# A linear-attention and two-mixer kernel: clamps on GpSimd, an earlier third tile, low parts by TensorE and ScalarE

## The chip, the cores and the metric

One core of a Trainium2 chip runs the whole program. The metric is the device time of one execution in microseconds, as the median of several runs. The five engines are TensorE (PE; its weight loads are listed as PEld), VectorE (DVE), ScalarE (ACT), GpSimd (POOL) and SyncE (SP), which issues the DMAs.

## The reference

The program has three parts. The first is a linear attention with decay: 4 batches, 8 heads, 768 steps, head size 48. The second is a mixer with a convolution over three steps and a gate. The third is a normalised residual mixer. All of it is in 32-bit floats.

```python
for t in range(S):
    cur = np.einsum('bhd,bhe->bhde', u[None] * kt, vt)
    y[:, :, t] = np.einsum('bhd,bhde->bhe', rt, state + cur)
    state = w[None, :, :, None] * state + np.einsum('bhd,bhe->bhde', kt, vt)
# then, on x of 4 x 768 x 384
h = np.maximum(x @ w_in, 0.0)                      # 384 -> 1024
conv_out[s] = sum over k of conv_w[k] * h[s + k - 1]
x = h * sigmoid(conv_out) @ w_out                  # 1024 -> 384
xn = (x - mean) / sqrt(var + 1e-6) * g_ln
out = x + np.maximum(xn @ w_ch1, 0.0) @ w_ch2      # 384 -> 1536 -> 384
```

## The kernel before

**Tiles.** The attention runs over 24 tiles of 128 steps, six for each batch. Inside a tile it is turned into matrix products: `dps` are the dot products of keys and queries, `aT` is their masked copy, `pst` is the tile's part of the state, `sbds` is the state laid out for TensorE, and `yps` is the tile's result, transposed, in one PSUM bank. The first mixer takes eight blocks of three tiles (`mixer1`), the second six blocks of four (`mixer2`).

**Three products for one.** TensorE multiplies in a shorter float format (fp32r). So each operand is split into a high part and a low part, and each product is made of three matmuls: high by high, high by low, low by high. For a tile's result, ScalarE copies `yps` to `xh` (the rounding makes the high part), and then the low part `xl` is `yps - xh`. Tiles 4 and 5 already make `xl` in another way: TensorE adds `-1 * xh` to the same bank (the matrix `minus`), and ScalarE copies the rest out.

**Weights.** The weights are split in the same way, but a program makes their rounding by hand, since they come in a packed form of two words: `magnitude` (line 122) has ScalarE take the absolute value and another engine clamp it; `decode` (line 129) has VectorE shift and merge bits in three steps; then ScalarE writes the high part and VectorE the low part. These steps are the generator `steps` of a weight job; `wdo(count)` advances the current job by so many steps (line 211), and a step that ends decoding calls the next job's `ahead`, so that the next magnitude is made early. Jobs 0 to 2 and 4 to 6 are parts of `w_in` (512 columns each), jobs 3, 7, 8 and 9 parts of `w_out` (768), and later jobs belong to the second mixer. Line 155 decides which engine clamps: VectorE for jobs 0 to 9, GpSimd from job 10 on.

**What sets the order.** A planner orders the instructions of each engine by its own costs, except those that are issued through `pe`, `vo`, `ao`, `go` and `so`: these keep the program's order on their engine. All matmuls, all of decoding with its ScalarE steps, and all of the first four tiles (`EARLY`) are of this kind; their line in the profile is the helper's, 77. In later tiles, ScalarE's and VectorE's steps are mostly left to the planner. An engine works its list strictly one after the other.

**The start.** `startup` (line 435) is written out by hand: `on(n)` runs the next part of tile n, `state_sum`, `state_update` and `decayed` do the state and the decayed keys, and `wdo` decodes weights between them. A light tile (n < 6) has four parts: the products `rk` and `z` on VectorE; dot products, mask and copies; `yps` and the `xh` copy; the low part and the halos. The others have three: `rk`, sums and `aT`; dot products and the masked copy; `yps`, `xh`, `xl` and the loads. After the start, `attention` (line 464) is a generator whose `go_on(n)` runs the next part of tile n; the first mixer advances it between its blocks of matmuls.

**PSUM.** The tag `pa` has three banks. `dps` (two), `yps` and `pst` of tiles from 4 on take turns in them.

Of the kernel before, what the change touches and what calls it, by code (L numbers as in the profile page):

```python
# [8 lines left out]
F32 = mybir.dt.float32  # L9
F32R = mybir.dt.float32r  # L10
I32 = mybir.dt.int32
AF = mybir.ActivationFunctionType
ALU = mybir.AluOpType
# [23 lines left out]
EARLY = 4  # L37
HAND = 9
LIGHT = 6
STEPS = (2, 4, 6, 8, 10, 12, 15), (1, 3, 4, 6, 7, 9, 10, 12, 14, 16)  # L40
GC = 16
GE = 4
# [8 lines left out]
def body(ctx, tc, r, k, v, w, u, w_in, conv_w, w_out, g_ln, w_ch1, w_ch2, rkT, krv, small, out):  # L51
# [13 lines left out]
    v_ = nc.vector  # L65
    a_ = nc.scalar
# [55 lines left out]
    def magnitude(st, n, engine=go):  # L122

        t = ap.tile([128, WN], F32, tag="wd", name="wdec", bufs=2)[:, 0:n]
        ao.activation(out=t, in_=words(st, n)[1].bitcast(F32), func=AF.Abs)
        engine.tensor_scalar(out=t, in0=t, scalar1=W_MIN, scalar2=W_MAX, op0=ALU.max, op1=ALU.min)
        return t
# [14 lines left out]
    def wjob(src, n, hi, lo, scale=None):  # L142

        st, mag = [], []

        def load():
            st.append(io.tile([128, 2 * WN], I32, tag="st" if me >= 4 else "first", name="st", bufs=3 if me >= 4 else 4))
            dst = st[0][:, 0:2 * n]
            if len(src.shape) == 3:
                dst = dst.rearrange("p (a n) -> p a n", a=src.shape[1])  # L150
            so.dma_start(out=dst, in_=src.bitcast(I32))

        def ahead():
            if not mag:
                mag.append(magnitude(st[0], n, vo if me < 10 else go))

        def steps():
            ahead()
            t = mag[0]
            yield from decode(st[0], n, t)  # L160
            if me + 1 < min(len(wjobs), w_loaded[0]):
                wjobs[me + 1][2]()
            if len(src.shape) == 3:
                t = t.rearrange("p (a n) -> p a n", a=src.shape[1])
            kw = {} if scale is None else {"scale": gl[:, scale:scale + 1]}
            ao.activation(out=hi, in_=t, func=AF.Copy, **kw)
            yield
            if scale is None:
                vo.tensor_tensor(out=lo, in0=t, in1=hi.bitcast(F32), op=ALU.subtract)
            else:  # L170
                vo.scalar_tensor_tensor(out=lo, in0=t, scalar=kw["scale"], in1=hi.bitcast(F32),
                                        op0=ALU.mult, op1=ALU.subtract)
        me = len(wjobs)
        wjobs.append((load, steps(), ahead))
        return len(wjobs) - 1

# [76 lines left out]
    def decayed_k(n):  # L253

        if n < LIGHT:
            vo.tensor_tensor(out=kks[:, n % 2, 0, :, 0:D], in0=loaded[n][1], in1=tku[:, 0], op=ALU.mult)
            return
        inputs(n).tensor_tensor(out=kks[:, n % 2, :, :, 0:D], in0=loaded[n][1].unsqueeze(1).to_broadcast([128, 2, H, D]), in1=tku,
                         op=ALU.mult)
# [29 lines left out]
    def halos(n, xh, xl):  # L289
        i, j = n % TPB, n // TT  # L290
        g_ = vo if n < EARLY else nc.gpsimd
        for t, e in ((xh, 0), (xl, 1)):
            if i == 0:
                g_.memset(t[:, :, 0:1].bitcast(F32), 0.0)
            if i == TPB - 1:
                g_.memset(t[:, :, T + 1:T + 2].bitcast(F32), 0.0)
            if n % TT == 0 and i > 0:
                g_.tensor_copy(out=xT[j - 1][e][:, :, T + 1:T + 2], in_=t[:, :, 1:2].bitcast(F32))
                g_.tensor_copy(out=t[:, :, 0:1], in_=xT[j - 1][e][:, :, T:T + 1].bitcast(F32))
# [68 lines left out]
    def attn_tile(n):  # L368
        b, i = divmod(n, TPB)
        rk, _, rt, vt, _ = loaded[n]  # L370
        py, py_tag = (ps_c, "acc") if n < EARLY else (ps_a, "pa")

        rT, kT = rk[:, 0], rk[:, 1]
        vo.tensor_tensor(out=rk, in0=rk, in1=trk, op=ALU.mult)
        if n < LIGHT:
            yield from light_tile(n, rk, vt, py, py_tag)
            return
        av = ap.tile([128, H, D], F32, tag="av", name="av", bufs=2)
        v_.tensor_tensor(out=av, in0=kks[:, n % 2, 1, :, 0:D], in1=rt, op=ALU.mult)
        a8 = sp.tile([128, H, 1], F32, tag="a8", name="a8", bufs=2)  # L380
        v_.tensor_reduce(out=a8.rearrange("x (q p) o -> x q (p o)", q=2), in_=av.rearrange("x (p q) d -> x q p d", q=2),
                         axis=AX.X, op=ALU.add)
        aT = ap.tile([128, 2, NP, C], F32, tag="aT", name="aT", bufs=2)
        for h in range(H):
            a_.activation(out=aT[:, h // NP, h % NP, :], in_=ident, func=AF.Copy, scale=a8[:, h, :])
        yield

        dps = dot_products(rT, kT)
        for q in range(2):
            v_.copy_predicated(out=aT[:, q], mask=later.bitcast(I32).unsqueeze(1).to_broadcast([128, NP, C]), data=dps[q])  # L390
        yield

        yps = py.tile([128, KT, C], F32, tag=py_tag, name="yps")
        products(n, yps, rT, vt, aT)
        j = n // TT
        xh, xl = xT[j] if j in xT else new_xT(j)
        sl = slice(1 + (n % TT) * C, 1 + (n % TT) * C + C)
        a_.activation(out=xh[:, :, sl], in_=yps, func=AF.Copy)
        v_.tensor_tensor(out=xl[:, :, sl], in0=yps, in1=xh[:, :, sl].bitcast(F32), op=ALU.subtract)
        load_tile(n + 3)  # L400
        if n + 2 < NT:
            decayed_k(n + 2)
        halos(n, xh, xl)
        finished[0] = n
        yield
# [3 lines left out]
    def state_sum(n):  # L409
        vt = loaded[n][3]  # L410
        if n % TPB != TPB - 1:
            pst = sums[n] = ps_a.tile([128, NP, D], F32, tag="pa", name="pst")
            for h in range(H):
                q0 = 64 * (h % 2)
                pe.matmul(pst[q0:q0 + 64, h // 2, :], lhsT=kks[:, n % 2, 0, h, :], rhs=vt[:, h, 0:D], start=True,
                          stop=True)

    def state_update(n):
        first, last = n % TPB == 0, n % TPB == TPB - 1
        v_, a_, g_ = ordered(n)  # L420
        if not last:
            pst = sums.pop(n)
            sn = ap.tile([PR, NP, D], F32, tag="sn", name="sn")
            if first:
                a_.activation(out=sn, in_=pst[0:PR], func=AF.Copy)
            else:
                v_.tensor_tensor(out=sn, in0=pst[0:PR], in1=state[0], op=ALU.add)
            if n % TPB < TPB - 2:
                state[0] = ap.tile([PR, NP, D], F32, tag="sw", name="sw")
                v_.tensor_tensor(out=state[0], in0=sn, in1=w128.to_broadcast([PR, NP, D]), op=ALU.mult)  # L430
            sb = sbd[(n + 1) % 2]
            a_.activation(out=sb[0:D, :, 0:D], in_=sn[0:D], func=AF.Copy)
            a_.activation(out=sb[64:PR, :, D:2 * D], in_=sn[64:PR], func=AF.Copy)

    def startup():

        tiles = {n: attn_tile(n) for n in range(EARLY + 1)}

        def on(n):
            next(tiles[n], None)  # L440

        decayed = decayed_k
        on(0), decayed(0), on(0)
        on(1), state_sum(0), state_update(0), decayed(1), on(1), state_sum(1)
        wdo(1)
        on(0), on(2), state_update(1), decayed(2)
        wdo(2)
        on(2), state_sum(2), on(0)
        wdo(1)
        on(1), on(3), state_update(2), decayed(3)  # L450
        wdo(2)
        on(3), state_sum(3), on(1)
        wdo(2)
        on(2), state_update(3)
        wdo(3)
        on(2), on(3)
        wdo(1)
        on(3)
        wdo(1)
        on(4), decayed(4)  # L460
        wdo(3)
        return tiles

    def attention(tiles):

        def go_on(n):
            if 0 <= n < NT:
                next(tiles.setdefault(n, attn_tile(n)), None)

        n = EARLY  # L470
        load_tile(n + 2)
        decayed_k(n + 1)
        go_on(n)
        yield
        for n in range(EARLY, NT):
            state_sum(n)
            state_update(n)
            go_on(n - 1)
            if n != LIGHT - 1:
                go_on(n + 1)  # L480
            yield
            go_on(n)
            if n == LIGHT - 1:
                yield
                go_on(n)
                go_on(n + 1)
                yield
            go_on(n + 1)
            yield

    def split_T(x, n, hi, lo, c0):
# [456 lines left out]
```

## Time and profile before

| | |
|---|---|
| median of 3 runs | 653.33 us |
| lowest and highest | 652.41 and 654.55 us |
| the profiled execution's own time | 653.91 us |
| its span, first to last instruction | 652.2 us |
| TensorE busy | 627.9 us, 96% of the span |
| VectorE busy | 421.7 us, 65% |
| ScalarE busy | 300.8 us, 46% |
| GpSimd busy | 81.2 us, 12% |
| the chain that ended last | TensorE 84%, VectorE 10%, ScalarE 2% |

The shares are means over very different stages. In the first hundred microseconds the attention's small steps, the weights' decoding and the first mixer run together; later there is little else than matmuls. So the profile is read by stages: busy times of each engine in windows, then the chain of waits, and then single instructions in order of time. A matmul's end is modelled; the spacing of starts tells more than its duration. PEclk is the share of TensorE's clock that was granted, 1.00 for 2.4 GHz and 0.5 for 1.2 GHz.

### The profile page before, as it was taken

The page shows a single profiled execution, that of the slowest core. Times are in us where ns is not written, and L with a number is a line of the kernel's source. Part 1 is how long each engine was busy: PE and PEld are TensorE (multiplying, and loading weights), DVE is VectorE, ACT ScalarE, POOL GpSimd, SP SyncE. Part 2 cuts the span into 40 slices and gives each one's busy share as a digit, 9 for nine tenths or more (in the row PEclk, how much of TensorE's full clock was granted, in tenths as well). Part 3 has the DMA queues.
Part 4 walks back from the last instruction along what each step waited for, and adds up shares of the span by engine and source line. Part 5 has one row for each costly group of instructions (what it writes and reads, how often), then busy time and mean ns, then how long its engine had stood idle before and what let it go on. Part 6 is the DMA issues. An engine that isn't in the chain of part 4 may idle for free.

```text
span 652.2 us, 11821 instructions
## 1 busy us (share of the span) xinstructions
PE 627.9 (96%) x4803; PEld 572.3 (88%) x4803; DVE 421.7 (65%) x793; ACT 300.8 (46%) x658; POOL 81.2 (12%) x108
## 2 busy tenths in 40 slices
PE   8969879999999999999999999999999999999996
PEld 5768868889999999999999999999999999999995
DVE  6989999999989999968978834314213422422111
ACT  3447677687687877766755511211211211211110
POOL 6312010110020001002115501001000100100000
PEclk8867989999999999999999999999999999999999
DMA  8934644444253524012125103002002001100001
GB/s 231 309 107 156 211 146 125 125 133 159 71 174 118 162 83 137 18 47 88 52 82 171 60 0 98 1 0 98 1 0 83 16 0 50 50 0 19 31 0 54
DMA packets 25296, 56.52 MB, mean 87 GB/s; under 512 B 2961, under 2 KB 15378, under 8 KB 25234
## 3 DMA queue, kind: packets, MB, share of 16 engines
q1 hardware_dynamic: 25234, 55.68, 27.1%
q8 instruction: 40, 0.66, 0.4%
q14 instruction: 22, 0.18, 0.1%
HBM read 46.24 MB, written 9.44 MB: 85 GB/s over the span
## 4 chain that ended last, share of the span: by engine, by line
PE 84%; DVE 10%; ACT 2%; issue 1%; DMA 1%; POOL 1%; SPq 0%; DVEq 0%; ACTq 0%; POOLq 0%
PE acc L77 36%; PE psm L77 36%; PE yps L77 5%; PE dps L77 4%; DVE wdec L77 3%; DVE c L541 2%; PE pst L77 2%; PE pxt L77 1%; DVE rk L77 1%; DMA x1b<-x_dram 1%; DVE c L522 1%; PE pa L77 1%; DVE gl L528 1%; DVE kks L77 0%; POOL tables L762 0%
## 5 line engine op out<-in xcount | busy, mean ns | idle before, releaser
L555 DVE SCALAR_TENSOR_TENSOR rl<-psm,rh 128x512 fp32r<-128x512 f32 x72 | 49.6, 689 | 136.0 <-ACT rh L554 132.5
L554 ACT ACTIVATE rh<-psm 128x512 fp32r<-128x512 f32 x72 | 43.1, 599 | 199.6 <-PE psm L77 199.5
L77 PE MATMUL acc<-c2h,rh 128*128 128x384 f32 x288 | 97.0, 337 | 0.0
L77 PE MATMUL acc<-c2l,rh 128*128 128x384 f32 x288 | 97.0, 337 | 0.0
L77 PE MATMUL acc<-c2h,rl 128*128 128x384 f32 x288 | 96.9, 336 | 0.0
L77 PE MATMUL psm<-xnh,c1h 128*128 128x512 f32 x216 | 86.6, 401 | 0.0
L77 PE MATMUL psm<-xnh,c1l 128*128 128x512 f32 x216 | 84.9, 393 | 0.0
L77 PE MATMUL psm<-xnl,c1h 128*128 128x512 f32 x216 | 84.7, 392 | 0.0
L541 DVE SCALAR_TENSOR_TENSOR c<-h,tables,c 128x384 f32<-128x384 f32 x128 | 78.5, 617 | 8.0 <-ACT c L539 7.5
L77 PE MATMUL psm<-xh,wih 128*128 128x386 f32 x192 | 69.8, 364 | 4.4 <-DVE xl L77 4.4
L77 PE MATMUL acc<-woh,gl 128*128 128x384 f32 x192 | 65.3, 340 | 4.4 <-DVE gl L528 4.4
L77 PE MATMUL acc<-woh,gh 128*128 128x384 f32 x192 | 67.4, 351 | 0.4 <-ACT gh L527 0.4
L77 PE MATMUL psm<-xl,wih 128*128 128x386 f32 x192 | 67.1, 350 | 0.0
L77 PE MATMUL psm<-xh,wil 128*128 128x386 f32 x192 | 66.9, 348 | 0.0
L77 PE MATMUL acc<-wol,gh 128*128 128x384 f32 x192 | 65.3, 340 | 0.0
L77 PEld LDWEIGHTS acc<-c2l,rh 128*128 128x128 f32 x288 | 54.0, 188 | 3.0
L77 PEld LDWEIGHTS acc<-c2h,rh 128*128 128x128 f32 x288 | 54.1, 188 | 2.8
L77 PEld LDWEIGHTS acc<-c2h,rl 128*128 128x128 f32 x288 | 54.0, 188 | 0.0
L77 PEld LDWEIGHTS psm<-xnh,c1l 128*128 128x128 f32 x216 | 40.6, 188 | 9.3
L77 POOL TENSOR_SCALAR wdec<-wdec 128x768 f32<-128x768 f32 (+1 forms) x13 | 35.7, 2749 | 103.4 <-ACT wdec L77 76.3
L77 PEld LDWEIGHTS psm<-xnl,c1h 128*128 128x128 f32 x216 | 40.6, 188 | 6.1
L77 PEld LDWEIGHTS psm<-xnh,c1h 128*128 128x128 f32 x216 | 40.6, 188 | 6.1
(132 smaller groups left out, 1107.9 us busy)
## 6 DMA issues: line engine op xcount, KB each, us to landing
rk<-in_rkT_dram SPq DMA_DIRECT2D x24, 448.0 KB, 4.5
st<-in_moe_w_ch_dram SPq DMA_DIRECT2D x12, 768.0 KB, 4.6
rv<-in_krv_dram SPq DMA_DIRECT2D x18, 448.0 KB, 4.7
kt<-in_krv_dram SPq DMA_DIRECT2D x24, 192.0 KB, 4.5
x_dram<-x SPq DMA_DIRECT2D x24, 192.0 KB, 1.9
x1b<-x_dram SPq DMA_DIRECT2D x24, 192.0 KB, 3.3
out_dram<-x1b SPq DMA_DIRECT2D x24, 192.0 KB, 2.0
st<-in_moe_w_in_dram SPq DMA_DIRECT2D x6, 512.0 KB, 9.4
```

What stands on the lines that cost most here:

```text
L77: return lambda *args, **kw: tc.keep_in_program_order(op(*args, **kw))
L522: v_.tensor_tensor(out=st["c"], in0=st["h"][:, 1:T + 1], in1=st["c"], op=ALU.mult)
L528: v_.tensor_tensor(out=st["gl"], in0=st["c"], in1=st["gh"].bitcast(F32), op=ALU.subtract)
L541: v_.scalar_tensor_tensor(out=c, in0=h[:, o:o + T], scalar=cw[:, tap, f:f + 1], in1=c, op0=ALU.mult, op1=ALU.add)
L554: a_.activation(out=gh[:, 0:cols], in_=ps[:, 0:cols], func=AF.Relu)
L555: v_.scalar_tensor_tensor(out=gl_[:, 0:cols], in0=ps[:, 0:cols], scalar=0.0, in1=gh[:, 0:cols].bitcast(F32), op0=ALU.max, op1=ALU.subtract)
```

## The change

There are three edits. The clamps of weight jobs 6 to 9 go from VectorE to GpSimd. In `startup`, the third part of tile 0 (`yps`, `xh`) and the first part of tile 2 (`rk`, `z`) are put ahead of the first step of the first weight job. Tiles 6 to 9 make their low part as tiles 4 and 5 do, by the matrix `minus` and a ScalarE copy; this is a fourth part of the tile, which `attention` runs right behind the second part of the next tile.

```diff
+MID = 10
@@ wjob, ahead
-                mag.append(magnitude(st[0], n, vo if me < 10 else go))
+                mag.append(magnitude(st[0], n, vo if me < 6 else go))
@@ attn_tile
         a_.activation(out=xh[:, :, sl], in_=yps, func=AF.Copy)
-        v_.tensor_tensor(out=xl[:, :, sl], in0=yps, in1=xh[:, :, sl].bitcast(F32), op=ALU.subtract)
         load_tile(n + 3)
         if n + 2 < NT:
             decayed_k(n + 2)
+        if n < MID:
+            yield
+            pe.matmul(yps, lhsT=minus, rhs=xh[:, :, sl], start=False, stop=True, skip_group_check=True)
+            a_.activation(out=xl[:, :, sl], in_=yps, func=AF.Copy)
+        else:
+            v_.tensor_tensor(out=xl[:, :, sl], in0=yps, in1=xh[:, :, sl].bitcast(F32), op=ALU.subtract)
         halos(n, xh, xl)
@@ startup
         on(1), state_sum(0), state_update(0), decayed(1), on(1), state_sum(1)
+        on(0), on(2)
         wdo(1)
-        on(0), on(2), state_update(1), decayed(2)
+        state_update(1), decayed(2)
         wdo(2)
@@ attention
             go_on(n + 1)
+            if LIGHT <= n < MID:
+                go_on(n)
             yield
```

## Rows read from the trace of the kernel before

**Rows 1.** Windows: length, busy us of PE, PEld, DVE, ACT, POOL; PEclk, DMA, GB/s.
```profile
20.00:40.00 20.00, 15.19 (x267) 12.52 (x263) 18.42 (x35) 11.12 (x25) 6.19 (x8) 0.89 0.78 234
60.00:80.00 20.00, 18.21 (x144) 17.43 (x143) 20.00 (x32) 13.96 (x26) 2.53 (x3) 0.93 0.56 181
80.00:100.00 20.00, 16.13 (x148) 14.40 (x149) 19.30 (x34) 13.24 (x34) 2.85 (x3) 0.91 0.47 146
200.00:220.00 20.00, 20.00 (x226) 18.87 (x225) 18.87 (x34) 14.43 (x38) 0.21 (x2) 1.00 0.48 152
```

**Rows 2.** Chain of waits, 13 to 45 us: start, us, engine and tile.
```profile
19.65 0.49 ACT xh L77
...
21.51 0.43 DVE wdec L77
...
40.11 3.25 PE psm L77 x9
```

**Rows 3.** Timeline of TensorE: start, us, engine, line, instruction [idle before <-releaser].
```profile
80.14 1.16 PE L77 MATMUL dps<-rk 48*128 48x128 f32 x16 [1.93 <-ACT c L539]
...
89.70 0.45 PE L77 MATMUL acc<-woh,gl 128*128 128x384 f32 x1 [3.30 <-DVE gl L528]
```

**Rows 4.** Timeline of ScalarE and VectorE, 15 to 20 us.
```profile
15.38 0.68 ACT L77 ACTIVATE wdec<-st 128x512 f32<-128x512 f32 x1
...
16.09 0.99 DVE L77 TENSOR_SCALAR wdec<-wdec 128x512 f32<-128x512 f32 x2 [2.89 <-ACT wdec L77]
...
17.00 1.22 DVE L77 TENSOR_TENSOR rk<-rk,tables 112x1024 f32<-112x1024 f32 x1
...
18.93 0.35 DVE L77 TENSOR_TENSOR sn<-pst,sw 112x192 f32<-112x192 f32 x1
...
19.65 0.49 ACT L77 ACTIVATE xh<-yps 128x384 fp32r<-128x384 f32 x1 [3.60 <-PE yps L77]
...
20.06 1.41 DVE L77 SCALAR_TENSOR_TENSOR wdec<-st,wdec 128x512 int32<-128x512 int32 x2
```

**Rows 5.** Timeline of TensorE, 8 to 25 us: equal groups at two clocks.
```profile
8.70 1.16 PE L77 MATMUL dps<-rk 48*128 48x128 f32 x16 [0.86 <-DVE rk L77]
...
11.38 1.96 PE L77 MATMUL dps<-rk 48*128 48x128 f32 x16
...
17.05 1.71 PE L77 MATMUL yps<-aT,rv 128*32 128x128 f32 x32
...
23.22 1.06 PE L77 MATMUL yps<-aT,rv 128*32 128x128 f32 x32
```

**Rows 6.** Timeline of VectorE's clamps and a product; then groups: busy, mean ns, idle before.
```profile
52.94 0.42 DVE L77 TENSOR_SCALAR wdec<-wdec 128x512 f32<-128x512 f32 x1
...
61.77 1.18 DVE L77 TENSOR_SCALAR wdec<-wdec 128x768 f32<-128x768 f32 x1
...
76.02 0.55 DVE L77 TENSOR_SCALAR wdec<-wdec 128x768 f32<-128x768 f32 x1
...
82.76 0.96 DVE L522 TENSOR_TENSOR c<-h,c 128x384 f32<-128x384 f32 x1
...
L77 POOL TENSOR_SCALAR wdec<-wdec 128x768 f32<-128x768 f32 x12 | 35.4, 2953 | 103.4 <-ACT wdec L77 76.3 <-PE psm L77 27.0
...
L522 DVE TENSOR_TENSOR c<-h,c 128x384 f32<-128x384 f32 x64 | 35.3, 556 | 8.9 <-ACT c L521 8.7
```

**Rows 7.** Timeline of TensorE and ScalarE around `minus`, dot products and `xh`.
```profile
64.06 0.34 PE L77 MATMUL yps<-xh,minus 128*128 128x384 f32 x1
...
64.23 0.34 PE L77 MATMUL psm<-xh,wih 128*128 128x386 f32 x1
...
104.25 1.16 PE L77 MATMUL dps<-rk 48*128 48x128 f32 x16 [0.38 <-ACT gh L527]
...
106.33 0.47 ACT L398 ACTIVATE xh<-yps 128x384 fp32r<-128x384 f32 x1
...
122.82 1.16 PE L77 MATMUL dps<-rk 48*128 48x128 f32 x16 [0.97 <-PE yps L77]
```

## The prediction

> **What bounds the kernel now.** I read the stages first. In [rows 1] TensorE is busy for the whole 20 us of the window at 200 us, and from 143 us on nearly all windows look so: a matmul added there counts in full, and a faster VectorE wins nothing there. Before that the picture is another: between 20 and 40 us VectorE works 18.4 of 20 us and TensorE 15.2, and from 60 to 80 us VectorE is busy without a gap. So I read the chain of waits for the two early stretches. In the start-up [rows 2] it runs from the first tile's copy `xh` on ScalarE (19.65) over ScalarE's magnitude of the second weight block into VectorE's clamp (21.51) and along VectorE to the first big matmul at 40.11. A second look, at the chain from 50 to 89.7 us, shows VectorE alone, one instruction behind the other, until the matmul of 89.70 in [rows 3]. From there on TensorE carries the chain, with short waits. Hence three regions: to 90 us each microsecond of VectorE's list counts in full; from 90 to 143 us only the short waits of TensorE are to be had; later every matmul that is added counts in full.
>
> **Part 1, the start-up order.** `on(0), on(2)` now stand ahead of the first `wdo(1)`. These instructions move: tile 0's products on TensorE, its `xh` copy on ScalarE, tile 2's `rk` and `z` on VectorE. No DMA is issued in either block, so SP's and GpSimd's queues keep their order. TensorE's order doesn't change, since the block that is passed has no matmul. VectorE's does: `rk` and `z` take 1.93 us (17.00 to 18.93) [rows 4], and they now fall into the 2.89 us in which VectorE waits for ScalarE's magnitude. That is the gain that one sees at once, and it would be worth up to 1.93 us.
> But ScalarE's order changes too. All of these instructions are kept in program order on their engine. Before, the magnitude of weight block 0 runs at 15.38, while ScalarE would only wait (3.60 us) for tile 0's products; `xh` comes after it, at 19.65 [rows 4]. Now `xh` is ahead of the magnitude in ScalarE's queue, and the magnitude, with sbds, the second magnitude and all behind it, waits for the products. Worked out: `xh` starts at 19.65 and holds ScalarE for 0.49, the magnitude takes 0.68, so the clamp can start at 20.8 instead of 16.09. Behind it VectorE still has clamp and shift (16.09 to 17.00, 0.91), then sn, sw and kks (18.93 to 20.06, 1.13). So the instruction that starts at 20.06 now starts at 20.8 + 0.91 + 1.13 = 22.84, **2.8 us later**. VectorE, with 1.93 us less to do, idles for five. What covers this? From 20.06 to 40.1 VectorE has hardly a gap, and TensorE, ScalarE and GpSimd wait for it in turns, so nothing takes the delay up: the first big matmul, and VectorE's list behind it, move by 2.8 us. The moved rk and z may run longer beside GpSimd's work for tile 1; five idle us hide that.
> The delay has a lower end. The products end late because TensorE runs at 1.2 GHz ahead of them: the 16 dot products of tile 0 take 1.16 us and those of tile 1 1.96; 32 products of tile 0 take 1.71 and those of tile 1, later, 1.06 [rows 5]. At 2.4 GHz these two groups would be 1.45 us faster, and the two small groups between them, slowed alike, some 1.2: about 2.7 together. The magnitude would then start near 17.4, and the delay would be about 0.1. The instructions up to that point are the same as before, so I expect the same clock and take 2.8; ends 0.1 and 3.3 (TensorE now idles 1.4 us for kks and may fall back to 1.2 GHz later).
>
> **Part 2, clamps of blocks 6 to 9 by GpSimd.** VectorE loses four instructions: 0.42, 1.18, 0.55 and 0.55 us (the third is like the fourth), 2.70 in all, all on its gapless chain [rows 6]. The 1.18 is a 0.55 instruction that ran beside GpSimd's work; that stretch falls on another instruction afterwards. So 2.07 are safely removed. GpSimd needs 2.95 us for each. This latency is hidden: each magnitude is made when the block ahead has been decoded, 6 to 10 us before the shift that needs it, and GpSimd is nearly idle. The exception is block 7, where tile 5's select and product hold GpSimd; if its clamp comes behind them, VectorE's shift may wait, and everything on VectorE behind it.
> What comes back is the quarrel with GpSimd over memory: beside a GpSimd clamp a product that takes 0.556 on the mean took 0.96 at 82.76 [rows 6], 0.41 more, once in the 2.77 us; beside other clamps I see nothing. So 0 to 4 x 0.41 = 1.64 comes back; I take half, 0.8, as both kinds of rows occur. Net gain 1.2, ends 0.4 and 2.7. On the chain to 89.7 this counts in full, as a shorter wait of TensorE at 80.14 (1.93) [rows 3].
> The Trainium skill (GPSIMD Engine Reference, Key points) says that GpSimd shares its SBUF interfaces with VectorE, in contention with VectorE instructions in a 2-port mode or with two SBUF inputs. The trace agrees with it in the 0.96 above. Read as a tax on the whole clamp it is a rival, below.
>
> **Part 3, low parts of tiles 6 to 9.** VectorE loses four subtractions. TensorE gains four matmuls; one costs what lies between its start and the next, 64.06 to 64.23, 0.17, so 0.7 us in all [rows 7]. ScalarE gains four copies, each like its `xh` copy. The point is the place: `go_on(n)` follows `go_on(n+1)` at once, so TensorE's order is products(n), dot products(n+1), minus(n), and minus waits for ScalarE's `xh`. All of TensorE's matmuls queue behind it. For tile 7, dot products run from 104.25 to 105.4, while `xh` ran at 106.33 to 106.8, behind eight aT copies: TensorE would wait 1.4 us. For tile 6 the copy is done in time. So 0 to 1.4 per tile; two tiles late and each about half of that, as the wait also lets VectorE catch up: 1.3. On the other side the waits of TensorE for VectorE's `rk` in this stretch (0.38 at 104.25, 0.97 at 122.82, same rows) should shrink as VectorE has less to do; I take 1.2 with the small ones. Net 0.7 + 1.3 - 1.2 = 0.8 slower, ends -1.0 and +5.1 (no gain, 1.4 each at three tiles). ScalarE's copies lie beside matmuls; the bank of yps is released later, which the next state sum would feel.
>
> **Sum.** The profiled execution took 653.91 us (span 652.2 and 1.7 around it). 653.91 + 2.8 - 1.2 + 0.8 = 656.3. It is 0.6 above the median of 653.33, so the forecast for the median is **655.7**, own range 653.8 to 657.6.
>
> **Rivals.** (a) TensorE at full clock in the start-up: the delay is 0.1 instead of 2.8, time 653.0. Against it: the same instructions ran at 1.2 GHz before. 0.15. (b) The other side: the planner, which orders the instructions not held in program order by its own costs, puts `gl` early enough that the wait of 3.30 us at 89.70 goes [rows 3], and with it the fall of the clock: in 80 to 100 us it is 0.91 on the mean [rows 1], about 1.8 us lost, of which I count 1.5. 4.8 us less, time 650.9. It decides as soon as `gl` no longer stands behind two predicated copies and decoding steps. For it: VectorE's load in this stretch changes, so the order is made anew; against it: VectorE's relief alone, at most 2.7, is used up by the wait of 1.93 first. 0.14. (c) The change doesn't do what it says: ScalarE's magnitude keeps its place ahead of `xh`; then 1.93 are won in place of 2.8 lost, time 651.0. 0.08. (d) minus waits for `xh` at three tiles with 1.4 each and VectorE's relief brings nothing back: 655.7 - 0.8 + 4.9 = 659.8. 0.08. (e) GpSimd slows each VectorE instruction beside it by 0.41 in 0.55, for all of 4 x 2.77 us: about 4.7 lost for 2.07 gained, 2.6 slower where I have 1.2 faster, time 659.5. The rows show one slowed instruction in a clamp, not all: 0.05. By the sentence of the Trainium skill above it would be this one, if all instructions there had two SBUF inputs.
>
> **How the numbers follow.** The forecast has 0.50. About 0.3%, 2.0 us, can be told from no change: faster is under 651.3, slower over 655.3. Faster: most of (b) and (c), 0.16. Same: (a), the rest of (b) and (c), and the lower 0.18 of the forecast, 0.38. Slower: the rest of the forecast, (d) and (e), 0.46. The range 651.0 to 659.5 takes in the forecast, (a) and the nearer parts of the others, and leaves about 0.2 out.
>
> **What would show it.** In the profile after: ScalarE's first magnitude behind `xh`, near 20.1, VectorE idle about 5 us before the first clamp, and the first matmul of psm near 42.9 instead of 40.1; if it comes before 41, part 1 is wrong. Part 2: no VectorE clamps after block 5, the wait near 80 us short, two-input products of 0.9 us beside GpSimd. Part 3: minus directly behind the dot products, with a wait for `xh` ahead of it at tiles 7 and 8. After 145 us nothing should differ but the start. The forecast is most wrong if the clock in the first 20 us, or the planner's order near 85 us, comes out another way.

## The result, and the profile after

The changed kernel is slower: 658.01 us (median of 22 runs, 654.56 to 661.53) against 654.53 us for the kernel before in the same runs. The ratio is 1.0061 with a 95% interval of 1.0045 to 1.0076, which is 4.0 us (2.9 to 5.0). The forecast was 2.4 us more than before. The profiled execution took 655.42 us, span 653.7; it is one of the kernel's faster ones, and that turns out to matter.

First the start. Timelines of ScalarE, VectorE and TensorE of the changed kernel (start, us, engine, line, instruction, then in brackets the idle time before it and what ended it); they answer [rows 2, 4, 5].

```profile
14.62 1.08 PE L78 MATMUL yps<-aT,rv 128*32 128x128 f32 x32
15.10 0.93 DVE L78 TENSOR_TENSOR z<-rk 112x512 f32<-112x512 f32 x1
16.60 0.49 ACT L78 ACTIVATE xh<-yps 128x384 fp32r<-128x384 f32 x1 [2.05 <-PE yps L78]
17.12 0.67 ACT L78 ACTIVATE wdec<-st 128x512 f32<-128x512 f32 x1
17.82 0.89 DVE L78 TENSOR_SCALAR wdec<-wdec 128x512 f32<-128x512 f32 x2 [1.80 <-ACT wdec L78]
19.76 1.41 DVE L78 SCALAR_TENSOR_TENSOR wdec<-st,wdec 128x512 int32<-128x512 int32 x2
33.72 0.49 ACT L78 ACTIVATE xh<-yps 128x384 fp32r<-128x384 f32 x1 [3.38 <-PE yps L78]
35.83 0.56 DVE L78 TENSOR_SCALAR wdec<-wdec 128x768 f32<-128x768 f32 x1 [2.48 <-ACT wdec L78]
40.86 0.66 PE L78 MATMUL psm<-xh,wih 128*128 128x386 f32 x1 [4.43 <-DVE xl L78]
```

The magnitude now starts 0.52 behind `xh`, and VectorE, which has tile 2's `z` behind it at 16.0, waits for it. But `xh` itself is early, at 16.60 in place of 19.65: the 32 products of tile 0 began at 14.62 and not at 17.05 [rows 5], and took 1.08 and not 1.71 us. So the merge of 20.06 [rows 4] (the step of decoding that joins the bits of a weight) is not late at all here, at 19.76.

The first `psm` is still 0.75 late, for a reason further on. In the old order too, a later magnitude stands behind a later `xh` in ScalarE's queue, and the kernel before already waits there:

```profile
35.08 0.56 DVE L77 TENSOR_SCALAR wdec<-wdec 128x768 f32<-128x768 f32 x1 [1.29 <-ACT wdec L77]
```

In the changed kernel this wait is 2.48: that `xh` comes at 33.72, where it came at 32.96, and TensorE's granted clock is 0.50 from 26 to 32 us, after waits of 1.25 us for `kks` at 19.90 and of 1.57 us for `rk` at 24.99.

The windows of the changed kernel show the clock (length, busy us of PE, PEld, DVE, ACT, POOL; PEclk, DMA, GB/s). They answer [rows 1], with a window for the start.

```profile
8.00:20.00 12.00, 10.01 (x148) 8.69 (x148) 9.96 (x15) 6.03 (x16) 6.72 (x8) 1.00 1.06 329
20.00:40.00 20.00, 14.85 (x245) 12.34 (x245) 17.28 (x30) 9.40 (x21) 6.04 (x8) 0.81 0.87 276
60.00:80.00 20.00, 20.00 (x147) 19.56 (x148) 19.43 (x29) 13.75 (x28) 10.19 (x6) 0.83 0.40 124
80.00:100.00 20.00, 17.05 (x144) 15.34 (x144) 19.25 (x33) 15.05 (x38) 3.08 (x3) 0.83 0.55 164
200.00:220.00 20.00, 20.00 (x226) 18.86 (x225) 19.94 (x35) 14.23 (x36) 0.21 (x2) 1.00 0.47 146
```

And the same window of the kernel before:

```profile
8.00:20.00 12.00, 11.30 (x128) 9.54 (x130) 8.87 (x14) 4.94 (x13) 5.45 (x8) 0.72 1.05 302
```

From 8 to 20 us the granted clock is 1.00 after and 0.72 before, with the same matmuls in the same order. From 60 to 100 us it is the other way round, 0.83 after against 0.93 and 0.91. VectorE has no more room than before, 19.43 and 19.25 of 20 us, although four clamps have left it. And from 60 to 80 us it is now TensorE that is busy without a gap, 20.00 of 20 us, where it had 18.21.

TensorE's waits after 59 us, with the `xh` copy that one of them waits for; these answer [rows 3, 7].

```profile
59.90 1.41 PE L78 MATMUL pa<-ub,z 112*128 112x2 f32 x6 [1.98 <-DVE z L78]
83.94 2.08 PE L78 MATMUL dps<-rk 48*128 48x128 f32 x16 [2.70 <-issue]
97.74 0.44 PE L78 MATMUL yps<-xh,minus 128*128 128x384 f32 x1 [0.25 <-ACT xh L399]
105.68 1.16 PE L78 MATMUL dps<-rk 48*128 48x128 f32 x16 [0.26 <-issue]
107.67 0.48 ACT L399 ACTIVATE xh<-yps 128x384 fp32r<-128x384 f32 x1
108.20 0.45 PE L78 MATMUL yps<-xh,minus 128*128 128x384 f32 x1 [1.36 <-ACT xh L399]
116.88 0.45 PE L78 MATMUL yps<-xh,minus 128*128 128x384 f32 x1
```

The waits of 1.93 and 3.30 us are gone; others stand in their place. `minus` of tile 7 waits 1.36 us, that of tile 6 0.25, those of tiles 8 and 9 (116.88 and 125.56) not at all.

How far the changed kernel lags shows in the first matmul of each group of `psm`, which are the same in both: 0.75 us at the first, 0.09 at the next two, 3.0 at the groups from 67 to 80 us, 6.0 at the group of 88.99, and 1.1 from 145 us on, where it stays to the last group at 320 us. VectorE's list can be followed in the merges, whose order is the same in all kernels: the one that stood at 43.62 is 0.75 late, the one that stood at 87.63 not at all (0.02 early). Here is one such matmul of the changed kernel, which stood at 187.70 before:

```profile
188.82 0.34 PE L78 MATMUL psm<-xh,wih 128*128 128x386 f32 x1
```

So the profiled execution of the change has a start that was hardly delayed, no delay of VectorE's list is left in it at 88 us, and it shows only a part of the 4.0 us. Which edit costs what had to come from kernels with the edits apart.

### The profile page after: what moved, and what is told of

The parts are those of the page before. It is cut to its first block, busy times and chain, and to the rows that moved or that the text cites. A ratio compares the mean times of both kernels' runs of the same rounds, so it can differ in the third digit from the quotient of the medians.

```text
span 653.7 us, 11839 instructions
## 1 busy us (share of the span) xinstructions
PE 630.2 (96%) x4807; PEld 575.0 (88%) x4807; DVE 422.5 (65%) x785; ACT 302.2 (46%) x662; POOL 92.0 (14%) x112
## 4 chain that ended last, share of the span: by engine, by line
PE 75%; DVE 15%; issue 3%; ACT 3%; DMA 2%; POOL 1%; SPq 0%; ACTq 0%; POOLq 0%
PE acc L78 33%; PE psm L78 32%; PE yps L78 4%; DVE wdec L78 3%; PE dps L78 3%; DVE c L550 2%; DMA x1b<-x_dram 1%; DVE rk L78 1%; PE pst L78 1%; PE pxt L78 1%; PE pa L78 1%; DVE gl L537 1%; DVE c L531 1%; DVE aT L391 1%; ACT aT L386 1%
## 5 line engine op out<-in xcount | busy, mean ns | idle before, releaser
L550 DVE SCALAR_TENSOR_TENSOR c<-h,tables,c 128x384 f32<-128x384 f32 x128 | 80.4, 632 | 7.0 <-ACT c L548 6.5
L78 POOL TENSOR_SCALAR wdec<-wdec 128x768 f32<-128x768 f32 (+2 forms) x17 | 47.7, 2808 | 96.7 <-ACT wdec L78 67.9
```

The source lines that it names most:

```text
L78: return lambda *args, **kw: tc.keep_in_program_order(op(*args, **kw))
L550: v_.scalar_tensor_tensor(out=c, in0=h[:, o:o + T], scalar=cw[:, tap, f:f + 1], in1=c, op0=ALU.mult, op1=ALU.add)
```

## Experiments

**The three edits alone.** First the start order alone:

```diff
+        on(0), on(2)
         wdo(1)
-        on(0), on(2), state_update(1), decayed(2)
+        state_update(1), decayed(2)
```

> Only the start-up order is changed. Theory A (ScalarE's queue: the first magnitude waits behind xh for the products of tile 0): slower by 0.7 to 2.8 us, by TensorE's clock ahead of xh; where the profile shows xh near 19.6, the first psm matmul comes near 42.9 (before 40.1), where it shows xh near 16.6, near 40.9. On the mean +2 us. Rival B (the loss comes from the stretch at 80 to 90 us, from the moved clamps or low parts): this kernel is within 0.7 us of before.

Measured: 661.34 us, ratio 1.0111 (1.0088 to 1.0134), 7.3 us. The timelines of TensorE, ScalarE and VectorE of this kernel:

```profile
18.18 1.94 PE L77 MATMUL yps<-aT,rv 128*32 128x128 f32 x32
21.49 0.49 ACT L77 ACTIVATE xh<-yps 128x384 fp32r<-128x384 f32 x1 [5.01 <-PE yps L77]
22.01 0.66 ACT L77 ACTIVATE wdec<-st 128x512 f32<-128x512 f32 x1
22.70 0.89 DVE L77 TENSOR_SCALAR wdec<-wdec 128x512 f32<-128x512 f32 x2 [6.18 <-ACT wdec L77]
24.64 1.41 DVE L77 SCALAR_TENSOR_TENSOR wdec<-st,wdec 128x512 int32<-128x512 int32 x2
43.95 0.66 PE L77 MATMUL psm<-xh,wih 128*128 128x386 f32 x1 [4.44 <-DVE xl L77]
```

And its window of the start, as above:

```profile
8.00:20.00 12.00, 11.14 (x117) 9.12 (x114) 7.80 (x9) 4.13 (x11) 5.33 (x7) 0.62 1.05 332
```

The magnitude is again 0.52 behind `xh`, but here TensorE's clock is 0.62 ahead of it, `xh` is at 21.49, VectorE waits 6.18 us, and the merge and the first `psm` are 4.6 and 3.8 us later than before. The merges of 43.62 and 87.63 are still 3.8 and 3.7 late, so VectorE's list carries the delay on. The expectation of 0.7 to 2.8 us had the sign and the start right, but the time is far beyond it; the rest comes up below.

Then the clamps alone:

```diff
-                mag.append(magnitude(st[0], n, vo if me < 10 else go))
+                mag.append(magnitude(st[0], n, vo if me < 6 else go))
```

> Only the four clamps go to GpSimd. Step of the prediction: 1.2 us faster (0.4 to 2.7). Rival from the profile after, where four VectorE instructions beside the clamps took 0.4 to 0.6 us longer each, about 2.1 in sum: what is removed (2.07) comes back whole, and the time is within 0.5 us of before; then the first psm matmul stays at 40.1 and the groups at 64 to 83 us move by less than 0.5.

Measured: 657.16 us, ratio 1.0054 (1.0033 to 1.0076), 3.5 us slower, where I had 1.2 faster and the rival no change within 0.5: neither came out.

Then the low parts alone, the rest of the diff (`MID`, the fourth part of the tile, `go_on(n)` in `attention`):

> Only the low parts of tiles 6 to 9 are changed. Step of the prediction: 0.8 us slower (-1.0 to +5.1): 0.7 for four matmuls, waits for xh at one or two tiles (0.2 and 1.4 in the profile after), and shorter waits for rk. Rival: as VectorE is relieved by 2.2 us, TensorE's waits at 104, 107 and 122 us go and the kernel is 0.5 to 1.5 us faster.

Measured: 652.94 us, ratio 0.9985 (0.9965 to 1.0006), so 1.0 us faster, as the rival said, though no change lies within the interval too. TensorE's only waits from 90 to 130 us are these:

```profile
106.56 0.67 PE L78 MATMUL pst<-rv,kks 128*64 128x48 f32 x16 [0.41 <-DVE aT L391]
...
113.56 0.44 PE L78 MATMUL yps<-xh,minus 128*128 128x384 f32 x1 [0.21 <-ACT xh L399]
```

**The parts don't add.** 7.3 + 3.5 - 1.0 is 9.8, and the whole change is 4.0. The likeliest reason is the planner. In the traces the start edit alone puts 37 of VectorE's 793 instructions in another place of its order, the clamps 34, the low parts 15, and all three 37 (each time the fewest that must be moved to turn one order into the other). For the start edit, all but two of them lie at 52 us or later, far from the edit. SyncE's order never changes. So each edit was also measured beside the others.

The whole change without the start edit:

> The whole change without its start-up order. If the three parts added up, +3.2 for the clamps and -1.0 for the low parts: 2.2 us slower than before, and the start-up order alone (+7.4) would make 9.6 for the whole change, which measured 3.5. If the parts act through the planner's order, the sum doesn't hold: by the whole change less 0.7 to 2.8 us for the start, between 0.7 and 2.8 slower than before.

The whole change with the clamps left on VectorE (start order and low parts):

> Start order and low parts, clamps of blocks 6 to 9 left on VectorE. The parts alone gave 1.0111 and 0.9985, the whole change 1.0061. If the low parts' relief of VectorE is what takes back some of the start order's delay: near 1.006. If the parts add: 1.0096. If the clamps on GpSimd are what takes it back: 1.010.

The whole change with the low parts left on VectorE (start order and clamps):

> Start order and clamps, low parts of tiles 6 to 9 left on VectorE. The parts alone gave 1.0111 and 1.0054. If they add: 1.0165. If the low parts are what takes back the delay in the whole change: 1.012 or more. If the clamps are: near 1.007.

Measured, as ratios to the kernel before with their intervals, and in us of 654.5:

| edits | ratio | us |
|---|---|---|
| clamps | 1.0054 (1.0033 to 1.0076) | +3.5 |
| low parts | 0.9985 (0.9965 to 1.0006) | -1.0 |
| clamps, low parts | 0.9997 (0.9984 to 1.0010) | -0.2 |
| start | 1.0111 (1.0088 to 1.0134) | +7.3 |
| start, clamps | 1.0076 (1.0046 to 1.0106) | +5.0 |
| start, low parts | 1.0071 (1.0049 to 1.0094) | +4.6 |
| start, clamps, low parts | 1.0061 (1.0045 to 1.0076) | +4.0 |

The start edit costs 7.3, 1.5, 5.6 and 4.2 us, by what stands beside it: 4.7 on the mean. The clamps cost 3.5, 0.8, -2.3 and -0.6, 0.4 on the mean, with no sign of their own. The low parts give -1.0, -3.7, -2.7 and -1.0. Each of these is a difference of two ratios, good to 1.3 to 2.5 us by their intervals: the start edit's loss is clear in three places of four (not beside the clamps alone), the clamps' only where they stand alone, the low parts' gain in two. My two guesses on who takes the delay back were meant to exclude each other, and both came out: with the start edit, the clamps alone bring the time to 1.0076 (guessed 1.007) and the low parts alone to 1.0071 (guessed 1.006). For clamps and low parts I had expected 0.7 to 2.8 us of loss, and there is none. In the whole change the loss is that of the start edit, since without it the other two are at 0.9997.

The traces show where the start edit's extra loss arises when the clamps stay on VectorE. From the kernel with the start edit alone:

```profile
92.16 0.72 DVE L390 COPY_PREDICATED aT<-tables,dps 128x512 f32<-128x512 int32 x1
92.77 0.54 DVE L523 TENSOR_TENSOR c<-h,c 128x384 f32<-128x384 f32 x1
94.78 0.69 PE L77 MATMUL acc<-woh,gh 128*128 128x384 f32 x1 [5.89 <-ACT gh L528]
```

The planner has put the gate's product `c`, which stood at 82.76 [rows 6], behind both predicated copies; TensorE waits 5.89 us for the `gh` that is made from it, and the next group of `psm` is 7.6 us late, while VectorE's merges near it are only 3.7 late. The start edit with the low parts has the same order there and the same wait, 5.89. With the clamps moved too (start and clamps, whole change) the product stands ahead of the copies, and no wait of TensorE there is over 2.72 us. So, by the traces, the difference comes from the planner's order and not from the start.

**Which half of the start edit.** The edit moves two things, tile 0's `yps` and `xh`, and tile 2's `rk` and `z`. Here only the second goes ahead, once alone, once with the low parts, once with all the rest:

```diff
+        on(2)
         wdo(1)
-        on(0), on(2), state_update(1), decayed(2)
+        on(0), state_update(1), decayed(2)
```

> Tile 2's rk and z ahead of the first weight job, but tile 0's products and xh behind it as before. Theory A: no delay of the magnitude, so no loss; VectorE is 1.9 us ahead at 18 us, but the second clamp still waits for ScalarE's second magnitude, which follows xh and sbds: the first psm matmul stays at 40.1 if TensorE is slow ahead of xh, and up to 1.9 earlier if it isn't. Time 0 to 1.9 us faster. Rival (the moved rk and z are themselves the harm, by running beside GpSimd's work): slower by about what e1_order loses.

> The low parts of tiles 6 to 9 as in the change, and tile 2's rk and z ahead of the first weight job while xh stays behind it. Its orders are those of e3_low but for the two moved instructions. Expected 0 to 1 us faster than e3_low, 1.0 to 2.0 faster than before: the fastest of the versions so far.

> All three edits, but in the start only tile 2's products rk and z go ahead of the first decoding step; tile 0's yps and its copy xh stay behind it. Theory A (the loss of the whole change comes from xh standing ahead of the first magnitude in ScalarE's queue): first magnitude near 14 to 16 us whatever TensorE's clock does, psm near 38.5 to 39.5, ratio 0.997 to 1.000, as with clamps and low parts alone (0.9997), whose orders it shares but for two rows. Theory B (the loss comes from tile 2's products moving ahead, or from the sum of all edits): ratio near 1.006, as the whole change.

Measured: alone 653.52 us, ratio 0.9995 (0.9981 to 1.0009); with the low parts 653.78, 0.9985 (0.9968 to 1.0002); with the low parts and clamps 654.22, 1.0011 (0.9993 to 1.0029). Each shares its orders with the kernel that it extends (before, low parts, clamps and low parts) but for two rows on VectorE. The last one is the test: it differs from the whole change by one thing in the text, that `yps` and `xh` of tile 0 stay behind the first decoding step (the planner then also puts 30 of VectorE's instructions in other places), and 0.5% of the 0.61% are gone. The other two pairs say the same: 1.0111 against 0.9995 for the start alone, 1.0071 against 0.9985 with the low parts. The timeline of the kernel with all the rest:

```profile
14.12 0.68 ACT L78 ACTIVATE wdec<-st 128x512 f32<-128x512 f32 x1
18.32 0.49 ACT L78 ACTIVATE xh<-yps 128x384 fp32r<-128x384 f32 x1 [3.52 <-PE yps L78]
18.70 1.40 DVE L78 SCALAR_TENSOR_TENSOR wdec<-st,wdec 128x512 int32<-128x512 int32 x2
38.05 0.66 PE L78 MATMUL psm<-xh,wih 128*128 128x386 f32 x1 [5.27 <-DVE xl L78]
```

The magnitude starts at 14.12, 4.2 us ahead of `xh`, and the wait of VectorE for it is filled by `rk` and `z`. So it is `xh` ahead of the magnitude that costs, as the first theory said. The rival, that `rk` and `z` do the harm or the sum of all edits does, is out. What share of the cost is the delay itself, and what share the planner's order that comes with it, these pairs don't tell. Moving `rk` and `z` wins nothing that can be measured either: 0.9995, 0.9985 against 0.9985, 1.0011 against 0.9997. Beside it stands a warning: the profile of `rk` and `z` alone ends 2.1 us ahead of that of the kernel before, and the medians differ by 0.4. A lag read from a single profile is one draw too.

**Does a late magnitude pass on in full?** The kernel before, with the first magnitude written five times into the same place, and `xh` left behind it:

```diff
-    def magnitude(st, n, engine=go):
+    def magnitude(st, n, engine=go, times=1):
@@ magnitude
-        ao.activation(out=t, in_=words(st, n)[1].bitcast(F32), func=AF.Abs)
+        for _ in range(times):
+            ao.activation(out=t, in_=words(st, n)[1].bitcast(F32), func=AF.Abs)
@@ wjob, ahead
-                mag.append(magnitude(st[0], n, vo if me < 10 else go))
+                mag.append(magnitude(st[0], n, vo if me < 10 else go, 5 if me == 0 else 1))
```

> The kernel before, with ScalarE writing the first weight block's magnitude five times into the same place (4 x 0.68 = 2.7 us later); nothing else is edited, xh stays behind it. Theory A (a delay of the first magnitude passes on in full, nothing between it and the first big matmul takes it up): first merge near 22.7, psm near 42.8, time +2.7 us, ratio 1.004, within 0.003 for the order that the planner makes anew later. Rival (VectorE's list of the start has slack): psm under 41, ratio 1.000.

Measured: 655.71 us, ratio 1.0033 (1.0015 to 1.0052), 2.2 us (1.0 to 3.4).

```profile
14.34 3.51 ACT L77 ACTIVATE wdec<-st 128x512 f32<-128x512 f32 x5
17.88 0.89 DVE L77 TENSOR_SCALAR wdec<-wdec 128x512 f32<-128x512 f32 x2 [4.46 <-ACT wdec L77]
19.50 0.49 ACT L77 ACTIVATE xh<-yps 128x384 fp32r<-128x384 f32 x1 [1.65 <-PE yps L77]
21.74 1.41 DVE L77 SCALAR_TENSOR_TENSOR wdec<-st,wdec 128x512 int32<-128x512 int32 x2
31.97 0.43 DVE L77 TENSOR_SCALAR wdec<-wdec 128x512 f32<-128x512 f32 x1 [1.37 <-ACT wdec L77]
42.91 0.66 PE L77 MATMUL psm<-xh,wih 128*128 128x386 f32 x1 [4.44 <-DVE xl L77]
```

`xh` stands where it stood before (19.50), the clamp is 1.8 later (17.88 for 16.09; the first magnitude itself began 1.0 earlier than before, at 14.34), the merge 1.7 (21.74 for 20.06, where I had expected 22.7), and the first `psm` 2.8 (42.91 for 40.11). Nothing on the way took the delay up. It even grew, since VectorE now waits 1.37 us at 31.97 for a later magnitude, where the kernel before has no wait. The merge of 87.63 is 2.1 late, and from 145 us on this kernel lags by 2.0.

**The clamps: contention or order?** The same as the clamps alone, but the four clamps are not computed by any engine; VectorE's and ScalarE's orders are then, row for row, those of the clamps alone. The clamps of weight blocks 6 to 9 are the part that this kernel leaves out.

```diff
-                mag.append(magnitude(st[0], n, vo if me < 10 else go))
+                mag.append(magnitude(st[0], n, vo if me < 6 else None if me < 10 else go))
@@ magnitude
-        engine.tensor_scalar(out=t, in0=t, scalar1=W_MIN, scalar2=W_MAX, op0=ALU.max, op1=ALU.min)
+        if engine is not None:
+            engine.tensor_scalar(out=t, in0=t, scalar1=W_MIN, scalar2=W_MAX, op0=ALU.max, op1=ALU.min)
```

> The kernel before with the clamps of blocks 6 to 9 left out altogether (the limit on very small and very large weights is not applied there). VectorE's and ScalarE's orders are the same, row for row, as in e2_clamps; the only difference to it is that GpSimd has no such clamps. Theory C (contention: GpSimd's clamps slow VectorE by 0.4 to 0.6 us at each and are starved themselves, to 5.1 and 8.1 us, so that what VectorE is relieved of comes back): 2 to 3 us faster than e2_clamps, near before or up to 1 us faster. Rival D (the planner's new order of VectorE and ScalarE, which the edit brings, is the harm): about as slow as e2_clamps, 2 to 3 us over before.

Measured: 655.79 us, ratio 1.0016 (1.0001 to 1.0032), against 1.0054 with the clamps on GpSimd: the difference of 0.38%, 2.5 us and good to 1.7, is what four clamps on GpSimd cost beside the same order of VectorE and ScalarE. First VectorE and GpSimd with the clamps on GpSimd:

```profile
49.83 1.65 DVE L541 SCALAR_TENSOR_TENSOR c<-h,tables,c 128x384 f32<-128x384 f32 x2 [0.74 <-ACT c L539]
56.86 5.12 POOL L77 TENSOR_SCALAR wdec<-wdec 128x768 f32<-128x768 f32 x1 [4.49 <-ACT wdec L77]
59.26 1.18 DVE L541 SCALAR_TENSOR_TENSOR c<-h,tables,c 128x384 f32<-128x384 f32 x1
65.06 3.07 POOL L77 TENSOR_SCALAR wdec<-wdec 128x768 f32<-128x768 f32 x1
65.42 1.17 DVE L541 SCALAR_TENSOR_TENSOR c<-h,tables,c 128x384 f32<-128x384 f32 x1
72.31 8.07 POOL L77 TENSOR_SCALAR wdec<-wdec 128x768 f32<-128x768 f32 x1 [4.19 <-ACT wdec L77]
77.66 1.19 DVE L541 SCALAR_TENSOR_TENSOR c<-h,tables,c 128x384 f32<-128x384 f32 x1
91.62 0.94 DVE L77 TENSOR_TENSOR wol<-wdec,woh 128x768 fp32r<-128x768 f32 x1
```

and, without them, the same VectorE instructions but that of 59.26:

```profile
51.19 1.27 DVE L542 SCALAR_TENSOR_TENSOR c<-h,tables,c 128x384 f32<-128x384 f32 x2 [0.74 <-ACT c L540]
65.78 0.61 DVE L542 SCALAR_TENSOR_TENSOR c<-h,tables,c 128x384 f32<-128x384 f32 x1
77.46 0.62 DVE L542 SCALAR_TENSOR_TENSOR c<-h,tables,c 128x384 f32<-128x384 f32 x1
90.84 0.94 DVE L77 TENSOR_TENSOR wol<-wdec,woh 128x768 fp32r<-128x768 f32 x1
```

From the first to the last of these rows VectorE needs 41.79 us with the clamps and 39.65 without, for the same list without a gap: 2.14 us for four clamps, half a microsecond each. Beside each clamp one VectorE row is longer: by 0.37 (the second `c` in the row of 49.83), 0.57 (1.18 at 59.26, for the 0.61 that such a row takes undisturbed; without the clamps it ran beside tile 5's select), 0.56 and 0.57 us.

The merges show the rest of this edit's loss. On the kernel before, the kernel without the four clamps goes from 0.78 late at the merge of 43.62 to 1.09 early at that of 87.63, a gain of 1.9 us; the kernel with the clamps on GpSimd from 0.58 to 0.30 early, a loss of 0.3. So up to 88 us GpSimd's clamps give back just what was removed. But from there to 145 us both lose, 2.2 and 2.8 us, with TensorE waiting for `gh`, `gl` and `rk`. What the two have in common against the kernel before is the planner's new order. By these lags it is the larger part of the 3.5 us, but it was not tested by itself.

**A second look at the whole change:**

> The changed kernel once more, for a second profile. Theory A: the time goes with TensorE's clock ahead of xh. If xh of tile 0 is near 19.6 here, the first psm matmul is near 42.9 and the time near 658 to 660; if it is near 16.6 again, near 40.9 and 655.5. A time of 658 or more with an early xh would put the spread elsewhere.

Measured: 656.19 us in the profiled execution, `xh` at 16.69, magnitude at 17.21, first `psm` at 40.93, as expected for an early `xh`. So the two profiled executions of the whole change have TensorE at full clock in the start, and the three of the other kernels with the start edit (alone, with clamps, with low parts) do not: `xh` at 21.49, 20.87 and 21.23, VectorE waiting 6.18, 5.94 and 6.29 us, `psm` at 43.95, 43.20 and 43.59. The whole change with a slow start, from which its slower executions would come by this theory, was not caught in a profile.

## Why the prediction was right, and where its working was not

The sign and the edit that decides were right. The size was short: 2.4 us forecast, 4.0 (2.9 to 5.0) measured. That it was not further off is in part luck, since the terms of parts 2 and 3 were both wrong and cancelled. Step by step:

**What bounds the kernel.** For the kernel before the regions held in the main: the late magnitude put into it passed on in full to the first `psm` (2.8 us) and mostly to the end (2.0 in the profile, 1.0 to 3.4 in time), and from 145 to 320 us no lag changes by more than 0.5 us. But "VectorE alone" was too simple. Up to 40 us there is a second path, from TensorE's products over `xh` and a magnitude on ScalarE to VectorE, and it makes VectorE wait in the old order too (1.29 us at 35.08). And in the changed kernel TensorE is the engine without a gap from 60 to 80 us.

**Part 1** had the right mechanism and a short price: 2.8 forecast, 4.2 in the whole change (good to 1.3). The wait of five us for the magnitude was there, 5.9 to 6.3, in three of five profiles. The step that failed is "I expect the same clock". I took `xh` at 19.65 as a property of the kernel; it is one of a wide range. Over the profiles of kernels with the old order `xh` starts between 16.70 and 21.18, with the new order between 16.60 and 21.49, and TensorE's granted clock from 8 to 20 us goes with it, from 1.00 to 0.62. In the old order the magnitude doesn't wait for it and starts between 14.01 and 15.96, and the first merge lies between 18.53 and 20.64 (without the kernel with the late magnitude). In the new order every microsecond of it goes into the merge: 19.76 at a granted clock of 1.00, 24.64 at 0.62. The first `psm` shows what is left of that at the end of the start. At a clock of 0.99 to 1.00 it is at 39.77 in the old order (clamps and low parts) and 40.86 in the new; at 0.62 it is at 40.89 in the old (no clamps) and 43.95 in the new (start edit alone). The edit did not add a fixed 2.8; it tied the weights' decoding to TensorE's clock, for 1.1 us at the one and 3.1 at the other. So up to the first `psm` my ends of 0.1 and 3.3 hold, and the 2.8 is a price of the lower clock. What the time shows beyond that arises later, at least where it could be located: the 5.89 us wait for `gh`, in the planner's order.

**Rival (a)**, the full clock, came true in the two profiles of the whole change, with the magnitude at 17.12 (17.4 forecast). Its time did not: 655.42 and 656.19, not 653.0. The first `psm` was still 0.75 late, by the fall of the clock later in the start that the prediction names beside its upper end, and more came by 89 us and went again (6.0, then 1.1). How this later part is divided between the planner's new order and the clock of 0.83 from 60 to 100 us was not separated.

**Part 2** was wrong. Forecast 1.2 us won; measured from 3.5 lost to 2.3 won, by what stands beside it. The failing term is what comes back by contention: I took half of 4 x 0.41, 0.8, with 1.64 as the end, and it is 2.14. The row of 0.96 [rows 6] had shown the right mechanism, and "beside other clamps I see nothing" was the error: of the twelve GpSimd clamps of before only the one beside that row lies in the stretch that VectorE bounds, the other eleven run from 138 us on. One row of one should have been taken as the price, not halved. With 2.07 removed and 2.14 given back, nothing is left, and VectorE's busy time from 49 to 92 us was 42.08 before and 42.19 with the clamps alone. So contention explains that nothing was won. It does not explain a loss of 3.5: the kernel without the four clamps is relieved of 2.07 and still 0.16% slower than before, and what both lose after 88 us is a term that the prediction put at nothing, the planner's new order. The Trainium skill (GPSIMD Engine Reference, Key points) names VectorE instructions in a 2-port mode or with two SBUF inputs as those that contend, and the rows stretched beside the clamps have two SBUF inputs, `h` and `c`. Rival (e) had the mechanism at too high a price: one instruction for each clamp is slowed, not all beside it.

**Part 3** was 0.8 slower by forecast and is 1.0 faster alone, between 2.3 faster and 0.4 slower. The waits of `minus` were sized well, 0.25 and 1.36 us at tiles 6 and 7 for a forecast of 1.3 in all, but only in the whole change; alone there is one of 0.21. With that and 0.7 for the four matmuls, the relief of VectorE must have been about 1.9 (0.9 + 1.0), where I took 1.2; the planner's new order is in this number, and so is the interval. Rival (d), three tiles with 1.4 each, is out: one has it.

**The sum** of parts 2 and 3 was -0.4, and together they measured -0.2, with both terms wrong and of opposite sign. **Rival (b)**: the wait of 3.30 is gone from the changed kernel, but one of 2.70 stands at 83.94 and the clock from 80 to 100 us is 0.83 and not 0.91, so nothing is won. What it feared of the planner came the other way round: with the start edit alone `gh` is put later and costs a wait of 5.89. **Rival (c)** is out: the magnitude did go behind `xh`.

**What stays open.** The start edit costs 7.3 us alone and 1.5 beside the clamps, though the profiled starts are alike (`psm` at 43.95 and 43.20). The difference arises at the wait for `gh` between 88 and 95 us, where the planner's orders differ; a kernel with only that product put back was not tried. Open too are how the 4.2 us in the whole change are divided, since its slower executions have no profile, and why TensorE's clock in the start differs from one execution to the next.

## What to carry to other kernels

Before an instruction is moved ahead on one engine, list what stands behind it on the other engines of the same block: `rk` and `z` filled a wait of VectorE, but `xh`, moved with them, put ScalarE's magnitude behind a stretch of TensorE whose length varies with its clock. A start time in one profile is one draw; where it depends on a clock that varies, ask what the new order does at both clocks. And where a planner lays the rest anew, test an edit beside the others too, and look for the waits that its new order makes far away: alone the start edit cost 7.3 us, with the others 4.2.

## What the runs showed of the hardware that I had not expected

A GpSimd instruction can be held up beside a full VectorE far longer than it holds VectorE up. With the clamps alone the same 128x768 clamp took 2.77 us in one place (82.23) and 5.12 and 8.07 in others, while VectorE paid about 0.56 once. In the whole change the clamps took 2.84 to 3.21 us, and VectorE paid much the same, 0.39 to 0.63 for each. The Trainium skill (SBUF — State Buffer, SBUF: two separate sides) says that, of a GpSimd instruction and a VectorE instruction that contends with it, whichever starts first holds the shared ports for its whole instruction and the other blocks. The 8.07 us agrees with it for the GpSimd side. For VectorE the trace does not: beside the clamp of 72.31 the row of 77.66 took 1.19 in place of 0.62, 0.57 more, and not the whole 2.77 of a clamp; the next rows with two SBUF inputs ran at their usual length while the clamp went on to 80.38.

TensorE's clock in the first 20 us differs between executions with the same matmuls in the same order: 0.62 to 1.00 in the mean from 8 to 20 us over 14 profiles, which moves tile 0's `xh` by 4.9 us. Five of them (before, clamps, low parts, no clamps, clamps and low parts) have the same order on all of TensorE, VectorE, ScalarE and GpSimd up to 50 us, and still 0.72, 0.86, 0.72, 0.62 and 0.99. Nothing in the runs shows why.
